# Attention with beacon keys and a gated feed-forward: one rotation of PSUM pairs, a later value phase, and casts moved between engines

## The chip, the cores and the metric

The kernel runs on one core of a Trainium2 chip. The metric is the device time of one launch in microseconds (us), the median of several runs. Its engines work at once and meet at semaphores: TensorE (PE; its weight loads PEld), VectorE (DVE), ScalarE (ACT), GpSimd (POOL) and SyncE (SP, which here only issues DMAs). TensorE writes into PSUM, eight banks of 512 float32 per partition.

## The reference

For 8 batches of 8 heads with 576 queries of 64 dimensions, 16 beacon keys and values are put in front of the 576 others; the mask is causal except for the beacons. The 4608 tokens of 512 values then go through a feed-forward.

```python
scores = scale * np.matmul(q, k_all.transpose(0, 1, 3, 2))
scores = np.where(causal, -1000000000.0, scores)
a = np.exp(scores - scores.max(-1, keepdims=True))
a /= a.sum(-1, keepdims=True) + 1e-09
attn = np.matmul(a, v_all)
x = attn.transpose(0, 2, 1, 3).reshape(B * S, H * D)
return np.maximum(x @ w_gate, 0.0) * (x @ w_val) @ w_out
```

## The kernel before, in words

Everything is in bfloat16, with float32 sums. Scores are computed transposed (keys on the partitions). A *unit* (`Unit`, L363) is one tile of up to 1024 score columns: `qk` (L373) issues its matmuls (L382) into a *pair* of PSUM banks, and `exp` (L387) has ScalarE write the exponentials to SBUF (L390) and, where the tile crosses the diagonal, GpSimd set the forbidden ones to zero (L398, the mask). A *chunk* (`Chunk`, L403) is a set of queries for four heads: `av` (L412) issues the value matmuls and those with ones for the sums (L442), `invert` (L451) has VectorE form the reciprocals (L455), `scale` (L466) has it write the normed result, transposed, to `xT` (L471), and `note` (L476) keeps the range of the reciprocals (L478).

The feed-forward works on tiles of 512 tokens (`Ffn`, L481). `up` (L486) makes one of twelve rows of hidden units: four gate matmuls (L497), a relu by ScalarE (L501, or L512 where gate and value share a pair), four value matmuls (L509) and a product by VectorE (L513). `down` (L515) makes 128 tokens of output with twelve matmuls (L521), which ScalarE copies out (L524) and SyncE stores (L527).

The order is written out by hand: L769 loops over a plan of steps. A step of a batch has two or three units, the chunks whose units the step before finished (`due`), and some `up` and `down` taken from a queue. Batches 0 and 1 have seven steps with two units each, then steps of feed-forward alone; batches 2 to 7 have five steps with 3, 3, 3, 3 and 2 units. In the later batches' steps (L798 to L824) the order on TensorE is two units, the chunk's value phase, the third unit, then `up` and `down`; where no chunk is due, three units and then `up`. PSUM of the later batches (`join_banks`, L736) is two pools: three pairs `p` in turn for scores, gates, values and outputs (one bank of the pair is used for the last three), and one pair `o` for the value phase, or for a step's first unit where no chunk is due; there the first `up` puts gate and value in one pair (`joint`).

Inputs are fetched ahead. For batches 2 to 7 `fetch` (L745) loads three tiles per step (SyncE, L247), casts each `late` steps later (GpSimd, L267 for queries and keys, L262 for values), and one step behind that turns keys and queries by a DMA transpose (SyncE, L272). Raw tiles lie in ten buffers. Batch 1's keys and queries come by casting DMAs issued from GpSimd (L293) and are turned by TensorE (L304); its values are loaded by SyncE and cast by GpSimd (L713). Weights come by casting DMAs issued from GpSimd (`load_w`, L340, issue at L342; `load_wo`, L359, at L360); the last third and `wo` are issued behind a one-element memset by VectorE (L706). So GpSimd's one queue holds masks, casts and issues in program order, and SyncE's holds loads, turns and stores.

Of the kernel before, what the change touches and what calls it, by code (L numbers as in the profile page):

```python
# [161 lines left out]
def kernel(  # L162
# [15 lines left out]
    P = 128  # L178
# [151 lines left out]
    LOADS = ([("k", 0), ("q", 1), ("k", 1), ("q", 2), ("k", 2), ("q", 3), ("k", 3), ("q", 0),  # L330
              ("k", 4), ("q", 4)] + [("v", t) for t in range(NKT)])

    def pair():

        return pools["p"].tile([P, 2, 512], FP32, name="p")

    def bank():
        return pair()[:, 0] if "p" in pools else f_ps.tile([P, 512], FP32, name="f")

    def load_w(dst, src, n0, n1, groups=(0, 1)):  # L340
        for g in groups:
# [61 lines left out]
    class Chunk:  # L403
# [8 lines left out]
        def av(self):  # L412
            batch, g, cis = self.batch, self.g, self.cis
            if batch.b == 0 and g == 1 and cis[0] < 2:
                ab = f_ps.tile([P, 512], FP32, name="f")
                self.os = f_ps.tile([P, 512], FP32, name="f")
            elif batch.b == 1 or batch.b == g == 0:
                ab = o_ps.tile([P, 512], FP32, name="ab")
                self.os = o_ps.tile([P, 512], FP32, name="os")
            else:  # L420
                o = (s_ps.tile([P, 2, 512], FP32, name="s") if batch.b == 0 else
                     pools["o"].tile([P, 2, 512], FP32, name="o"))
                ab, self.os = o[:, 0], o[:, 1]
            self.ab = [ab.rearrange("p (x n) -> p x n", x=2)]
            if len(cis) > 1:
                n = CHUNKS[cis[1]][1]
                self.ab.append(self.os[:, self.n:self.n + 2 * n].rearrange(
                    "p (x n) -> p x n", x=2))
            s0 = 0
            for x, ci in enumerate(cis):  # L430
                cq0, nq, segs = CHUNKS[ci]
                for i, (kt, q0, n, _, _) in enumerate(sorted(segs, key=lambda x: x[0])):
                    e = batch.e.pop((g, ci, kt))
                    kr, stop = min(P, Stot - kt * P), i == len(segs) - 1
                    for part in range(3):
                        for hh in range(4):
                            rows = slice(hh * C, (hh + 1) * C)
                            c0 = (4 * g + hh) * D + part * C
                            w = ones[:kr, :] if part == 2 else batch.v[:kr, kt, c0:c0 + C]
                            o = (self.os[rows, s0:s0 + nq] if part == 2 else  # L440
                                 self.ab[x][rows, part])
                            nc.tensor.matmul(  # L442
                                o[:, q0 - cq0:q0 - cq0 + n], w, e[:kr, 2 * (hh % 2) + hh // 2],
                                start=(x == 0 and i == 0 and part != 1), stop=stop,
                                skip_group_check=True)
# [35 lines left out]
    class Ffn:  # L481
# [1 line left out]
        def __init__(self, m0):  # L483
            self.m0, self.h = m0, None

        def up(self, nf, c0, c1, spare, joint=False):  # L486
            n = c1 - c0
            if self.h is None:
                self.h = fsb.tile([P, NF, M_TILE], BF16, name="hT")
            x = xT[:, :, self.m0 + c0:self.m0 + c1]  # L490
            if joint:
                both = pair()
                g, u = both[:, 0], both[:, 1]
            else:
                g = bank()
            for ki in range(KM):
                nc.tensor.matmul(g[:, :n], wg[:, ki, nf * P:(nf + 1) * P], x[:, ki],  # L497
                                 start=(ki == 0), stop=(ki == KM - 1))
            gs = fsb.tile([P, M_TILE], FP32, name="g")
            if not joint:  # L500
                nc.scalar.activation(gs[:, :n], g[:, :n], AF.Relu)  # L501
            if joint:
                pass
            elif spare and "p" not in pools:
                u = s_ps.tile([P, 2, M_TILE], FP32, name="s")[:, 0]
            else:
                u = bank()
            for ki in range(KM):
                nc.tensor.matmul(u[:, :n], wv[:, ki, nf * P:(nf + 1) * P], x[:, ki],  # L509
                                 start=(ki == 0), stop=(ki == KM - 1))  # L510
            if joint:
                nc.scalar.activation(gs[:, :n], g[:, :n], AF.Relu)  # L512
            nc.vector.tensor_mul(self.h[:, nf, c0:c1], gs[:, :n], u[:, :n])  # L513

        def down(self, ms):  # L515
# [12 lines left out]

        def groups(self, c0, c1, d0, d1):
            t = (c1 - c0) * 8 / 2400  # L530
            return ([("up", t, lambda spare, joint=False, nf=nf: self.up(nf, c0, c1, spare, joint)) for nf in range(NF)]
                    + [("down", 2.6, lambda spare, ms=ms: self.down(ms)) for ms in range(d0, d1)])

    def rows_in_range():
# [6 lines left out]
        return ok  # L541

    def count_rows(ok):
        cnt_ps = pools["o"].tile([P, 2, 512], FP32, name="o")[:1, 0, :1]
# [21 lines left out]
    with tc.manual_schedule():  # L566
# [112 lines left out]
        between[3] = turn_first_tails  # L679
        behind[3] = lambda: [held.pop(0)() for _ in range(2)]  # L680
        after(1, lambda: first.cast("v", 2, pool))
        after(1, lambda: first.cast("v", 3, pool))
        mid[3] = lambda: load_w(wg, moe_w_gate, 256, 768)
        after(3, lambda: load_w(wv, moe_w_val, 256, 768, (0,)))
        after(4, lambda: first.cast("v", 4, pool))
        mid[5] = lambda: [cast_w(wg, raw_g, 256, g, pool) for g in range(2)]
# [23 lines left out]
            load_wo(6, 12)  # L710

        for t in range(NKT):
            after(s2 - 1 + (t + 2) // 2 * (t > 1), lambda t=t: second.cast("v", t, pool))  # L713

        def cast_small(x):
            x.beacon = x.cast_rows(x.beacon, dve)
# [19 lines left out]
        def join_banks():  # L736
            ps_ctx.close()
            pools["p"] = main.enter_context(
                tc.tile_pool(name="p_ps", bufs=3, space=bass.MemoryType.PSUM))
            pools["o"] = main.enter_context(  # L740
                tc.tile_pool(name="o2_ps", bufs=1, space=bass.MemoryType.PSUM))

        after(s2 + 1, close_wide)

# [6 lines left out]
                if u[0] != "v":  # L751
                    at(s + late + 1, lambda u=u: batches[b].turn(*u))

        fetch(2, s2 + 1, 2, True)
        for b in range(3, B):
            fetch(b, BASE[b] - (6 if b == 3 else 5))

        spans = [(m, m + M_TILE) for m in range(0, n_tokens, M_TILE)]
        queue, have, credit = [], 0, 0.0
# [9 lines left out]
        for s, (b, i, quota) in enumerate(plan):  # L769
# [26 lines left out]
                        notes.append(c.note)  # L796

            for j, u in enumerate(units):  # L798
                if len(units) > 2 and chunks and j == 2:
                    units[0].exp()  # L800
                    values()
                if len(units) > 2 and not chunks and j == 0:
                    u.qk(pools["o"].tile([P, 2, 512], FP32, name="o"))
                else:
                    u.qk()
                if j == 0 and s in between:
                    between[s]()
                if j == 0 and s in (3, s2 + 1):
                    values()
                if j == 0 and s == 0:  # L810
                    u.exp()
                    mid[s]()
            if units and s > 0:
                if not (len(units) > 2 and chunks):
                    units[0].exp()
                if s in mid:
                    mid[s]()
            if s in behind:
                behind[s]()
            if s not in (3, s2 + 1) and not (len(units) > 2 and chunks):  # L820
                values()
            if len(units) > 2:
                for u in units[1:]:
                    u.exp()  # L824
            if s == 7:
# [10 lines left out]
                credit -= mine[-1][1]  # L836
            if not mine:
                credit = 0.0
            other = units[1:] if len(units) == 2 else []
            for act_ in acts[:len(acts) // 2]:  # L840
                act_()
            acts = acts[len(acts) // 2:]
# [87 lines left out]
```

## Time and profile before

| | |
|---|---|
| median of 4 runs | 392.68 us (391.47 to 393.93) |
| the profiled execution | 393.93 us, its span 392.1 us |
| TensorE busy | 372.9 us (95%) |
| VectorE, ScalarE, GpSimd busy | 199.9, 190.4, 124.8 us |
| granted TensorE clock | 0.996 of full |
| DMA moved | 50.44 MB, 129 GB/s over the span |
| chain that ended last | 71% TensorE, 10% DMA, 6% GpSimd, 4% SyncE, 4% ScalarE |

The profile is of one execution, with times in us from its start. A row of a timeline names start, busy time, engine, line, operation, output<-input, shape and count, and in brackets how long the engine was idle before it and what ended that. Matmuls overlap, so that their busy times add to more than the clock; the distance from start to start is what they take.

### The profile page before, as it was taken

The page shows a single profiled execution, that of the slowest core. Times are in us where ns is not written, and L with a number is a line of the kernel's source. Part 1 is how long each engine was busy: PE and PEld are TensorE (multiplying, and loading weights), DVE is VectorE, ACT ScalarE, POOL GpSimd, SP SyncE. Part 2 cuts the span into 40 slices and gives each one's busy share as a digit, 9 for nine tenths or more (in the row PEclk, how much of TensorE's full clock was granted, in tenths as well). Part 3 has the DMA queues.
Part 4 walks back from the last instruction along what each step waited for, and adds up shares of the span by engine and source line. Part 5 has one row for each costly group of instructions (what it writes and reads, how often), then busy time and mean ns, then how long its engine had stood idle before and what let it go on. Part 6 is the DMA issues. An engine that isn't in the chain of part 4 may idle for free.

```text
span 392.1 us, 10193 instructions
## 1 busy us (share of the span) xinstructions
PE 372.9 (95%) x4297; PEld 188.1 (48%) x4297; DVE 199.9 (51%) x307; ACT 190.4 (49%) x270; POOL 124.8 (32%) x221
## 2 busy tenths in 40 slices
PE   7889898999979999999999999999999999999995
PEld 3454444544534455545554554555445544444443
DVE  4768466542643575347633674267525765412320
ACT  4763583337645553665356534654455613323321
POOL 1596564323444432352324242325320200000000
PEclk9999999999999999999999999999999999999999
DMA  8999999789869975696568755886210011002002
GB/s 217 215 184 174 194 195 220 153 171 210 140 135 217 200 148 131 169 186 117 108 167 183 146 105 138 181 131 138 79 55 2 2 56 53 2 28 82 1 27 87
DMA packets 148132, 50.44 MB, mean 129 GB/s; under 512 B 133616, under 2 KB 143600, under 8 KB 148080
## 3 DMA queue, kind: packets, MB, share of 16 engines
q1 hardware_dynamic: 139024, 44.48, 52.9%
q0 software_dynamic: 9056, 5.24, 10.0%
q8 instruction: 35, 0.57, 0.6%
q14 instruction: 17, 0.14, 0.1%
HBM read 38.34 MB, written 9.44 MB: 122 GB/s over the span
## 4 chain that ended last, share of the span: by engine, by line
PE 71%; DMA 10%; POOL 6%; SPq 4%; ACT 4%; issue 3%; DVE 1%; ACTq 0%; POOLq 0%
PE p L521 20%; PE p L497 17%; PE p L509 16%; PE o L442 6%; DMA raw<-in_k_dram 4%; PE p L382 4%; DMA raw<-in_v_dram 3%; DMA raw<-in_q_dram 2%; PE f L521 2%; PE f L497 2%; SPq L247 2%; ACT e L390 2%; DMA hwide<-in_k_dram 2%; POOL e L398 1%; PE s L509 1%
## 5 line engine op out<-in xcount | busy, mean ns | idle before, releaser
L513 DVE TENSOR_TENSOR hT<-g,p 128x512 bf16<-128x512 f32 x89 | 61.1, 688 | 108.8 <-PE p L509 72.1
L497 PE MATMUL p<-xT,wg 128*128 128x512 bf16 x356 | 91.5, 379 | 1.0 <-DVE hT L513 0.9
L509 PE MATMUL p<-xT,wv 128*128 128x512 bf16 x356 | 91.3, 379 | 0.0
L398 POOL TENSOR_SCALAR_AFFINE_SELECT e<-e 128x512 bf16<-128x512 bf16 (+2 forms) x80 | 46.2, 600 | 141.1 <-ACT e L390 141.1
L521 PE MATMUL p<-wo,hT 128*128 128x512 bf16 (+1 forms) x396 | 86.6, 376 | 0.0
L501 ACT ACTIVATE g<-p 128x512 f32<-128x512 f32 x82 | 49.3, 601 | 71.4 <-PE p L497 71.4
L390 ACT ACTIVATE e<-p 128x1024 bf16<-128x1024 f32 (+2 forms) x77 | 69.7, 960 | 14.7 <-PE p L382 14.1
L509 PEld LDWEIGHTS <-wv 128*128 128x128 bf16 x432 | 42.2, 98 | 51.4 <-issue 0.5
L521 PEld LDWEIGHTS <-hT 128*128 128x128 bf16 x444 | 42.4, 99 | 50.4 <-issue 3.9
L455 DVE RECIPROCAL r<-o 128x256 f32<-128x256 f32 (+1 forms) x24 | 47.0, 1958 | 34.8 <-PE o L442 34.8
L497 PEld LDWEIGHTS <-wg 128*128 128x128 bf16 x432 | 40.2, 97 | 51.1 <-issue 6.6
L524 ACT COPY ob<-p 128x512 f32<-128x512 f32 (+1 forms) x33 | 18.9, 574 | 67.5 <-PE p L521 64.8
L267 POOL CAST half<-raw 128x512 bf16<-128x512 f32 (+2 forms) x60 | 35.8, 622 | 24.3 <-DMA raw<-in_k_dram 15.0
L442 PEld LDWEIGHTS <-v 128*32 128x32 bf16 (+1 forms) x1408 | 27.1, 97 | 14.4 <-issue 9.6
L442 PE MATMUL o<-e,v 128*32 128x80 bf16 (+4 forms) x1056 | 29.6, 231 | 3.7 <-POOL e L398 2.8
L382 PEld LDWEIGHTS <-kT 64*128 64x128 bf16 x704 | 20.0, 96 | 22.0 <-issue 18.6
L262 POOL CAST v<-raw 128x512 bf16<-128x512 f32 (+1 forms) x40 | 24.9, 648 | 16.0 <-DMA raw<-in_v_dram 16.0
L390 ACT ACTIVATE e<-s 128x1024 bf16<-128x1024 f32 (+2 forms) x28 | 25.7, 967 | 6.3 <-PE s L382 6.3
L442 PE MATMUL o<-e,ones 128*32 128x80 bf16 (+4 forms) x528 | 24.2, 230 | 0.0
L382 PE MATMUL p<-qT,kT 64*128 64x80 bf16 (+3 forms) x476 | 24.1, 230 | 0.0
L497 PE MATMUL f<-xT,wg 128*128 128x512 bf16 x76 | 19.6, 380 | 0.3 <-DMA hwide<-in_k_dram 0.3
L501 ACT ACTIVATE g<-f 128x512 f32<-128x512 f32 x19 | 11.4, 599 | 16.5 <-PE f L497 16.5
(82 smaller groups left out, 249.1 us busy)
## 6 DMA issues: line engine op xcount, KB each, us to landing
out_dram<-ob SPq DMA_DIRECT2D x35, 256.0 KB, 2.3
raw<-in_q_dram SPq DMA_DIRECT2D x25, 256.0 KB, 4.4
raw<-in_v_dram SPq DMA_DIRECT2D x24, 256.0 KB, 4.3
raw<-in_k_dram SPq DMA_DIRECT2D x19, 256.0 KB, 4.4
raw<-in_v_dram SPq DMA_DIRECT2D x8, 224.0 KB, 3.6
wo<-in_moe_w_out_dram POOLq DMA_DIRECT2D x2, 768.0 KB, 12.9
raw<-in_k_dram SPq DMA_DIRECT2D x6, 224.0 KB, 3.5
raw<-in_v_dram SPq DMA_DIRECT2D x8, 160.0 KB, 4.6
```

The costliest lines, as they stand in the source:

```text
L262: copy(self.v[:n, t].rearrange("p (h a d) -> p h a d", a=2, d=C), raw[:n].rearrange("p (h d a) -> p h a d", a=2, d=C))
L267: copy(h[:n], raw[:n])
L382: nc.tensor.matmul(self.s[:, a, c + j * n:c + (j + 1) * n], kT[rows, 2 * g + j, k0:k0 + P], qT[rows, 2 * g + j, q0:q0 + n], start=True, st ...
L390: nc.scalar.activation(e[:, :k * 4 * n].rearrange("p (k a x) -> p a k x", k=k, a=2), self.s[:, :, :k * 2 * n].rearrange("p a (k x) -> p a ...
L398: nc.gpsimd.affine_select(out=cols[:, :, :m], in_=cols[:, :, :m], pattern=[[0, 4], [1, m]], compare_op=ALU.is_ge, fill=0.0, base=base, cha ...
L442: nc.tensor.matmul(o[:, q0 - cq0:q0 - cq0 + n], w, e[:kr, 2 * (hh % 2) + hh // 2], start=(x == 0 and i == 0 and part != 1), stop=stop, ski ...
L455: nc.vector.reciprocal(self.r[:, :self.n], self.os[:, :self.n])
L497: nc.tensor.matmul(g[:, :n], wg[:, ki, nf * P:(nf + 1) * P], x[:, ki], start=(ki == 0), stop=(ki == KM - 1))
L501: nc.scalar.activation(gs[:, :n], g[:, :n], AF.Relu)
L509: nc.tensor.matmul(u[:, :n], wv[:, ki, nf * P:(nf + 1) * P], x[:, ki], start=(ki == 0), stop=(ki == KM - 1))
L513: nc.vector.tensor_mul(self.h[:, nf, c0:c1], gs[:, :n], u[:, :n])
L521: nc.tensor.matmul(o[:, n], self.h[:, nf, ms * P:(ms + 1) * P], wo[:, nf, n], start=(nf == 0), stop=(nf == NF - 1))
```

## The change

PSUM of batches 2 to 7 becomes four pairs of names p0 to p3, and `pair` takes the one that was least recently taken. The value phase takes such a pair too, and single banks (`bank`) spare it until the next step's value phase begins. All units of a step are issued ahead of its value phase. The shared pair of gate and value goes. The casts of batch 2 come three steps behind their loads (two before), those of batch 3 two (one before), and their turns one step later with them. In batch 0 the cast of the fourth values goes from the end of step 1 to the middle of step 3, and the load of gate weights from there to the end of step 3. Batch 1's first two value tiles are cast by VectorE.

```diff
-    def pair():
-        return pools["p"].tile([P, 2, 512], FP32, name="p")
+    pairs, kept = list(range(4)), []
+
+    def pair(spared=()):
+        k = next(k for k in pairs if k not in spared)
+        pairs.remove(k)
+        pairs.append(k)
+        return pools["p"].tile([P, 2, 512], FP32, name=f"p{k}")
 
     def bank():
-        return pair()[:, 0] if "p" in pools else f_ps.tile([P, 512], FP32, name="f")
+        return pair(kept)[:, 0] if "p" in pools else f_ps.tile([P, 512], FP32, name="f")
...
-                o = (s_ps.tile([P, 2, 512], FP32, name="s") if batch.b == 0 else
-                     pools["o"].tile([P, 2, 512], FP32, name="o"))
+                if batch.b == 0:
+                    o = s_ps.tile([P, 2, 512], FP32, name="s")
+                else:
+                    o = pair()
+                    kept.append(pairs[-1])
...
-            if joint:
-                both = pair()
-                g, u = both[:, 0], both[:, 1]
-            else:
-                g = bank()
+            g = bank()
...
-        after(1, lambda: first.cast("v", 3, pool))
-        mid[3] = lambda: load_w(wg, moe_w_gate, 256, 768)
+        mid[3] = lambda: first.cast("v", 3, pool)
+        after(3, lambda: load_w(wg, moe_w_gate, 256, 768))
...
-            after(s2 - 1 + (t + 2) // 2 * (t > 1), lambda t=t: second.cast("v", t, pool))
+            after(s2 - 1 + (t + 2) // 2 * (t > 1), lambda t=t: second.cast("v", t, pool if t > 1 else dve))
...
-                tc.tile_pool(name="p_ps", bufs=3, space=bass.MemoryType.PSUM))
-            pools["o"] = main.enter_context(
-                tc.tile_pool(name="o2_ps", bufs=1, space=bass.MemoryType.PSUM))
+                tc.tile_pool(name="p_ps", bufs=1, space=bass.MemoryType.PSUM))
...
-        fetch(2, s2 + 1, 2, True)
+        fetch(2, s2 + 1, 3, True)
         for b in range(3, B):
-            fetch(b, BASE[b] - (6 if b == 3 else 5))
+            fetch(b, BASE[b] - (6 if b == 3 else 5), 2 if b == 3 else 1)
...
-                if len(units) > 2 and chunks and j == 2:
-                    units[0].exp()
-                    values()
-                if len(units) > 2 and not chunks and j == 0:
-                    u.qk(pools["o"].tile([P, 2, 512], FP32, name="o"))
-                else:
-                    u.qk()
+                u.qk()
...
             if units and s > 0:
-                if not (len(units) > 2 and chunks):
-                    units[0].exp()
+                units[0].exp()
...
-            if s not in (3, s2 + 1) and not (len(units) > 2 and chunks):
+            kept.clear()
+            if s not in (3, s2 + 1):
                 values()
-            if len(units) > 2:
+            if units and b >= 2:
                 for u in units[1:]:
                     u.exp()
...
-                if kind == "up" and j == 0 and len(units) > 2 and not chunks:
-                    run(False, True)
-                    continue
```

More of the change, by code (lines that the diff above doesn't have):

```diff
@@ L484, in __init__, with up @@
             self.m0, self.h = m0, None
-        def up(self, nf, c0, c1, spare, joint=False):
+        def up(self, nf, c0, c1, spare):
             n = c1 - c0
@@ L499, in up @@
             gs = fsb.tile([P, M_TILE], FP32, name="g")
[L500 to L504, printed above, removed]
+            nc.scalar.activation(gs[:, :n], g[:, :n], AF.Relu)
+            if spare and "p" not in pools:
                 u = s_ps.tile([P, 2, M_TILE], FP32, name="s")[:, 0]
@@ L510, in up @@
                                  start=(ki == 0), stop=(ki == KM - 1))
-            if joint:
-                nc.scalar.activation(gs[:, :n], g[:, :n], AF.Relu)
             nc.vector.tensor_mul(self.h[:, nf, c0:c1], gs[:, :n], u[:, :n])
@@ L530, in groups @@
             t = (c1 - c0) * 8 / 2400
-            return ([("up", t, lambda spare, joint=False, nf=nf: self.up(nf, c0, c1, spare, joint)) for nf in range(NF)]
+            return ([("up", t, lambda spare, nf=nf: self.up(nf, c0, c1, spare)) for nf in range(NF)]
                     + [("down", 2.6, lambda spare, ms=ms: self.down(ms)) for ms in range(d0, d1)])
@@ L543, in count_rows @@
     def count_rows(ok):
-        cnt_ps = pools["o"].tile([P, 2, 512], FP32, name="o")[:1, 0, :1]
+        cnt_ps = pair()[:1, 0, :1]
         nc.tensor.matmul(cnt_ps, ok, ones[:, :1], start=True, stop=True)
@@ L838 @@
                 credit = 0.0
-            other = units[1:] if len(units) == 2 else []
+            other = units[1:] if b in (0, 1) else []
             for act_ in acts[:len(acts) // 2]:
```

## The prediction

> **What bounds the kernel now.** I read the table by stages first, cut at the moments when a batch's first score unit starts.
>
> ```profile
> 40.00:88.00 48.00, 44.47 (x564) 22.36 (x562) 26.73 (x41) 24.14 (x35) 23.41 (x39) 1.00 1.03 188
> 88.00:128.00 40.00, 35.30 (x493) 18.32 (x493) 17.49 (x21) 24.07 (x31) 18.16 (x33) 0.96 0.86 178
> 209.20:249.72 40.52, 40.33 (x497) 20.48 (x496) 21.99 (x31) 21.55 (x30) 14.42 (x27) 1.00 0.68 147
> ```
>
> The first column after the stretch is its length, the next TensorE's busy time; the last three are granted clock, DMA share, GB/s. From 128 on TensorE is busy 40.33 of 40.52 us per batch: it is the bound, and only its gaps and the entries between kinds of matmul are left. Before 128 some 14 us are idle and the clock dips once. So I read TensorE's timeline for every gap (in brackets: idle before, and who ended it).
>
> ```profile
> 23.20 0.40 PE L442 MATMUL f<-e,v 128*32 128x256 bf16 x8 [0.77 <-POOL e L398]
> 49.47 0.39 PE L442 MATMUL ab<-e,v 128*32 128x240 bf16 x8 [1.19 <-POOL e L398]
> 61.94 1.46 PE L521 MATMUL f<-wo,hT 128*128 128x512 bf16 x6 [0.84 <-DMA wo<-in_moe_w_out_dram]
> 65.44 0.40 PE L442 MATMUL ab<-e,v 128*32 128x256 bf16 x8 [0.81 <-POOL e L398]
> 103.11 0.39 PE L442 MATMUL o<-e,v 128*32 128x240 bf16 x8 [0.90 <-DVE xT L471]
> 109.23 0.30 PE L442 MATMUL o<-e,v 128*32 128x128 bf16 x8 [0.36 <-POOL e L398]
> 116.32 0.33 PE L442 MATMUL o<-e,v 80*32 80x80 bf16 x8 [2.48 <-POOL e L398]
> 117.18 6.45 PE L521 MATMUL p<-wo,hT 128*128 128x512 bf16 x24
> 128.16 1.02 PE L497 MATMUL p<-xT,wg 128*128 128x512 bf16 x4 [0.19 <-DVE hT L513]
> ```
>
> Five of these end at a causal mask (L398) on GpSimd. GpSimd's own timeline says why the last was late:
>
> ```profile
> 111.97 0.60 POOL L267 CAST half<-raw 64x512 bf16<-64x512 f32 x1 [1.67 <-DMA raw<-in_q_dram]
> 114.63 1.21 POOL L262 CAST v<-raw 128x512 bf16<-128x512 f32 x2 [2.06 <-DMA raw<-in_v_dram]
> 115.79 0.47 POOL L398 TENSOR_SCALAR_AFFINE_SELECT e<-e 128x320 bf16<-128x320 bf16 x1
> ```
>
> The mask's input was ready at 109.4 (ScalarE's exps of 107.83), but it stood in line behind batch 3's casts, and those waited for loads. The chain of waits runs through the same load, cast and mask.
>
> **The change, part by part.** From the instruction order of both builds: ScalarE's order differs in one swap, TensorE's only in where value phases stand, and GpSimd's and SyncE's in casts and turns.
>
> *Batch 0's fourth values after the first mask, gate weights after the last.* At 19.19 GpSimd cast v3 (landed 19.13), then two masks to 21.0, two weight issues (20.95, 1.54 us), then the mask that TensorE needed, 22.51 to 23.15. Now the two masks (their exp ended 17.88) fit in the 1.53 us in which GpSimd sat idle before 19.19, v3 follows, the needed mask ends at 19.83 + 0.64 = 20.5: the 0.77 gap goes. VectorE's unbroken string from 23.93 to 27.83, which the first up-projection at 27.35 needs, moves with it: 0.8 us. The weight issues go about 0.5 us earlier, what follows them 1.0.
>
> *Batch 1's first two values by VectorE.* On GpSimd they took 1.25 us (47.63) ahead of the mask that TensorE awaited at 49.47: that gap of 1.19 goes. VectorE's casts of 128x512 take 0.43 us (L289), this strided one at most the 0.65 of GpSimd's L262: 0.9 to 1.3 us, in VectorE's idle 1.97 us before 46.67. Behind them stands the product at 46.67, for which TensorE waits at 47.41; cost there 0 if the values have landed by 44.5, up to 1 us else. I take 0, since the next gap covers it: at 61.94 TensorE waits for wo, which came 15.1 us after its issue (46.81) with the DMA engines saturated (share 1.03). So of all gained so far only what moves wo's landing survives. Its issue is gated by VectorE's memset at 42.77, behind TensorE's turns at 40.63, which wait for loads that GpSimd now issues 1.0 earlier. Bounds 0 and 1.0; I take 0.85, as the transfers were idle for 2 us at 27 to 29 waiting for exactly those issues.
>
> *Casts of batches 2 and 3 one step later.* Masks now precede casts that wait for loads. The gaps at 65.44 (0.81), 109.23 (0.36) and 116.32 go. The last is worth 2.65 us (the last matmuls would have started at 113.67). And the 24 down-projections behind it took 6.39 us against 5.29 elsewhere, with the granted clock at 0.50 in 116 to 118 and 0.64 in 118 to 120: 1.10 more. The Trainium skill speaks against this term: its page "TensorE: Matmul & The Clock Gate", section "Part 1: The HAM clock gate (the \"warmup\" mystery)", lets the clock fall to half only after an idle window of about 3.4 us. By that rule an idle of 2.48 us does not dip and nothing is to be had here (sum 4.96); by the row it did, behind a phase of small matmuls, and waits of 0.77 to 1.19 us did not. The row decides: 1.10.
>
> The price is on SyncE: turns (L272) now stand behind later loads. For batch 2 the turn of q3, issued until 80.78, gets 2.55 us of loads and stores put in front (2.08 for v2 to v4, 0.47 for a store), less the 0.85 lead: 82.5, landing 1.5 later at 84 (turns take 2.7 from issue to landing, 1.2 of it issue). TensorE wants it at 88.91 - 1.66 = 87.25. Covered. For batch 3 the first units want q3 by 112.31 - 1.8 = 110.5; it was issued until 108.86, gets 2.94 us of loads in front, gains the lead, and loses 1.6 and 1.0 us of waits for casts inside two turns: 108.3 to 111, landing 109.8 to 112.4. The last turn, q4, is wanted at 123.9 - 5.6 = 118.3; between 88 and 125 SyncE waited 10.6 us for GpSimd, so it lands between 114 (no waits left, held by a store that needs the second down-projection) and 122 (all left). The middle, 118, costs about 0.3; bounds 0 and 4.
>
> *Four pairs, least recently used; value phase behind three score units.* Each run of score matmuls pays an entry of about 0.11 us: four of 256 columns alone took 0.32 us (214.48 to 214.80), eight 0.54. One run fewer in three steps of a batch: 0.32 us. The pair that gate and value shared is gone; at 128.16 and its like the third gate waited 0.35 (start to start) for VectorE's product, and the new order makes it wait for ScalarE's relu of the first, 0.4 us earlier than needed: 0.35 gained, less 0.05 as the first value tile now waits for an exp that ends as it wants to start. Added waits: in the third and fourth steps the value phase takes the pair of the last up-projection's product.
>
> ```profile
> 212.92 0.69 DVE L513 TENSOR_TENSOR hT<-g,p 128x512 bf16<-128x512 f32 x1 [1.04 <-PE p L509]
> 213.21 0.40 PE L442 MATMUL o<-e,v 128*32 128x256 bf16 x8
> 221.99 0.69 DVE L513 TENSOR_TENSOR hT<-g,p 128x512 bf16<-128x512 f32 x1 [1.04 <-PE p L509]
> 222.36 0.39 PE L442 MATMUL o<-e,v 128*32 128x240 bf16 x8
> ```
>
> The product ends at 213.61, and TensorE started 0.06 after such an end at 209.20. The value phase, moved 0.21 behind a third unit, would want 213.42: 0.25 lost. In the next step product 222.68 against 222.56: 0.18, and 0.1 more as the wait sits on the weight load. Behind it queue the next up-projections; nobody else is late, as ScalarE already has its three exps. Per batch 0.32 + 0.30 - 0.53 = about 0.1, at most 0.6; five batches: 0.75 taken, -1 to 2. In batch 2 the 0.90 wait at 103.11 stays, now at the second score unit: 0.25 for its third step's value phase and 0.23 for the score units that now run behind that wait, against entries of 0.32, lose 0.16. The gap of 0.85 at batch 2's first unit (88.91) stays: the built program has its first score matmul wait for the same last product.
>
> **Sum.** 0.85 + 0.81 (65.44) + [0.36 + 2.65 + 1.10 - 0.16 - 0.3 = 3.65] + 0.75 = 6.06 us. The profiled execution took 393.93 (span 392.1): 387.9. It is the slowest of the four runs, 1.25 above the median, so 386.6 against 392.68. A difference of 0.5% (2 us) is about what this kernel's measurement can tell from none.
>
> **Rivals.** (1) The sum, 386.6: 0.58. (2) The turns take GpSimd's place: TensorE waits about 2 us for q4 of batch 3 near 118 and the clock dips as it did at 116: 3.1 given back, 389.7. For it: SyncE issues without a pause from 90 to 122 now; against: a third of that was waiting for casts. 0.20. (3) The pairs do not come free: each of the twelve value-phase waits 0.35 longer than the 0.25 above, 4 us: 390.6. For it: VectorE's reciprocals (1.76 and 2.16 us) stand ahead of products; against: at 212.92 VectorE had been idle 1.04. 0.12. (4) Slower: batch 2's loads of q4 and of the first values, now ahead of all its turns, are throttled as those issued at 53.84 (4.54 us) and 58.47 (3.43) were while wo was in flight. At 4 us each instead of 2.9 for all, q3's turn lands near 95, not 84, TensorE stands 7.4 us at 87.25 and pays 1.4 for the clock: 8.8 against 6.06, 395.4. It decides against the change if that turn lands after 93.3; against it, loads from 62 on took 0.8 to 1.2 each, wo having landed. 0.10.
>
> Range: (2) and (3) at the upper end, wo's lead of 1.0 and no wait for turns at the lower, with 2 us for the pairs: 383.8 to 391.2. Faster by over 0.5% (under 390.7): all of (1), most of (2) and half of (3), 0.79; within: 0.13; slower: 0.08.
>
> **What would show it.** Right: no GpSimd-ended gap over 0.3 us in TensorE's value phases; clock 1.00 from 110 to 125, 24 down-projections in 5.3 us there; batch period 40.2 to 40.5 after 128; third gate of a batch's second step without gap; value phases of the third and fourth steps with a VectorE-ended gap of 0.2 to 0.3. Wrong: a gap in front of score matmuls (L382, now another line) ended by a turn; wo's wait grown past 0.84 by all that was gained ahead of it; a batch period over 40.7.

## The result, and the profile after

The changed kernel takes 391.44 us in the median of 42 runs (388.58 to 393.77), the kernel before 392.75 in 63 runs: a ratio of 0.9967, 95% interval 0.9953 to 0.998. That is 0.8 to 1.8 us of gain where 6.1 were forecast; the time lies just above the range given. The profiled execution of after took 392.99 us (span 391.3, clock 0.989), slower than 37 of the 42.

The executions of one kernel scatter here with a standard deviation of 0.6 to 2.0 us. So a profile below shows a mechanism, and the ratios of many runs say what it is worth.

First the table by stages (columns as before); the third row is a batch of the later part.

```profile
40.00:88.00 48.00, 45.84 (x579) 23.16 (x578) 27.85 (x44) 24.81 (x37) 22.76 (x38) 1.00 1.00 191
88.00:128.00 40.00, 34.05 (x475) 18.06 (x474) 16.20 (x19) 22.22 (x30) 17.48 (x31) 0.91 0.91 173
192.23:232.48 40.25, 39.99 (x505) 20.73 (x497) 21.83 (x30) 21.50 (x31) 14.42 (x27) 1.00 0.69 147
```

The first stage became better: TensorE is busy 45.84 us instead of 44.47. A batch takes 40.25 instead of 40.52. But the stage between, where most of the gain was to come from, became worse: 34.05 instead of 35.30, the clock 0.91 instead of 0.96. TensorE's timeline of after shows where:

```profile
50.31 0.61 PE L511 MATMUL f<-xT,wv 128*128 128x512 bf16 x2 [0.23 <-DMA wv<-in_moe_w_val_dram]
51.26 0.60 PE L511 MATMUL f<-xT,wv 128*128 128x512 bf16 x2 [0.34 <-DMA wv<-in_moe_w_val_dram]
86.29 0.83 PE L388 MATMUL p<-qT,kT 64*128 64x256 bf16 x12 [0.85 <-DVE hT L513]
114.23 1.46 PE L388 MATMUL p<-qT,kT 64*128 64x256 bf16 x12 [4.52 <-DMA qT<-half]
117.67 6.59 PE L521 MATMUL p<-wo,hT 128*128 128x512 bf16 x24
213.41 0.40 PE L451 MATMUL p<-e,v 128*32 128x256 bf16 x8 [0.16 <-DVE hT L513]
```

All five gaps that GpSimd's masks ended are gone. In their place batch 3's first scores wait 4.52 us for a turn, that of q3, and run at half clock behind it. (L388 is the scores' line now, L451 the values', L511 the up-projections' value line; L521, L247, L262, L267 and L272 are what they were.) No mask is late any more; it now stands ahead of the casts that wait for loads, as intended:

```profile
105.38 0.61 POOL L267 CAST half<-raw 80x512 bf16<-80x512 f32 x1 [0.23 <-DMA raw<-in_k_dram]
106.73 0.48 POOL L404 TENSOR_SCALAR_AFFINE_SELECT e<-e 128x320 bf16<-128x320 bf16 x1 [0.74 <-ACT e L396]
109.39 0.60 POOL L267 CAST half<-raw 64x512 bf16<-64x512 f32 x1 [2.18 <-DMA raw<-in_q_dram]
```

The cast of q3 itself had ended by 101.8. What came late is its turn on SyncE's queue (start, time that the queue was held, what was issued; of the ten loads at the head only the first, the longest and the last are shown):

```profile
90.09 0.56 SPq L247 DMA_DIRECT2D raw<-in_beacon_k_dram  x1
92.40 3.34 SPq L247 DMA_DIRECT2D raw<-in_q_dram  x1
99.74 1.41 SPq L247 DMA_DIRECT2D raw<-in_k_dram  x1
101.33 1.20 SPq L272 DMA_TRANSPOSE kT<-half  x1
102.61 1.67 SPq L272 DMA_TRANSPOSE qT<-half  x1
104.38 1.22 SPq L272 DMA_TRANSPOSE kT<-half  x1
105.65 0.65 SPq L247 DMA_DIRECT2D raw<-in_q_dram  x1
106.35 0.61 SPq L247 DMA_DIRECT2D raw<-in_beacon_v_dram  x1
107.00 1.97 SPq L247 DMA_DIRECT2D raw<-in_v_dram  x2
109.07 1.23 SPq L272 DMA_TRANSPOSE qT<-half  x1
110.39 1.21 SPq L272 DMA_TRANSPOSE kT<-half  x1
111.70 1.22 SPq L272 DMA_TRANSPOSE qT<-half  x1
```

The last row is q3's. In the kernel before, the same load and the same turn stood so:

```profile
92.18 1.58 SPq L247 DMA_DIRECT2D raw<-in_q_dram  x1
107.64 1.22 SPq L272 DMA_TRANSPOSE qT<-half  x1
```

In after, from the first load of batch 3 at 90.09 to the end of q4's turn at 121.93 SyncE issues 29 DMAs without a pause, 31.8 us. TensorE wants q3 at 109.71.

### The profile page after: what moved, and what is told of

It is laid out like the page before. It is cut to its first block, busy times and chain, and to the rows that moved or that the text cites. A ratio compares the mean times of both kernels' runs of the same rounds, so it can differ in the third digit from the quotient of the medians.

```text
span 391.3 us, 10201 instructions
## 1 busy us (share of the span) xinstructions
PE 372.5 (95%) x4297; PEld 190.2 (49%) x4297; DVE 198.9 (51%) x309; ACT 190.0 (49%) x270; POOL 124.3 (32%) x219
## 4 chain that ended last, share of the span: by engine, by line
PE 83%; DMA 7%; DVE 3%; POOL 3%; issue 1%; SPq 1%; ACT 1%; DVEq 0%
PE p L521 20%; PE p L502 20%; PE p L511 20%; PE p L451 7%; PE p L388 3%; DMA wv<-in_moe_w_val_dram 3%; PE f L521 3%; DVE hT L513 3%; PE f L502 2%; PE s L388 1%; DMA hwide<-in_k_dram 1%; PE s L511 1%; PE f L304 1%; PE f L511 1%; POOL e L404 1%; PE ab L451 1%
## 5 line engine op out<-in xcount | busy, mean ns | idle before, releaser
L511 PE MATMUL p<-xT,wv 128*128 128x512 bf16 x356 | 91.3, 379 | 0.0
L505 ACT ACTIVATE g<-p 128x512 f32<-128x512 f32 x89 | 52.8, 603 | 71.4 <-PE p L502 71.3
L521 PE MATMUL p<-wo,hT 128*128 128x512 bf16 (+1 forms) x396 | 86.7, 377 | 0.0
L396 ACT ACTIVATE e<-p 128x1024 bf16<-128x1024 f32 (+2 forms) x84 | 75.2, 966 | 17.6 <-PE p L388 17.6
L464 DVE RECIPROCAL r<-p 128x256 f32<-128x256 f32 (+1 forms) x24 | 47.0, 1958 | 43.5 <-PE p L451 43.5
L511 PEld LDWEIGHTS <-wv 128*128 128x128 bf16 x432 | 42.0, 98 | 53.1 <-DMA wv<-in_moe_w_val_dram 2.2
L521 PEld LDWEIGHTS <-hT 128*128 128x128 bf16 x444 | 42.4, 98 | 48.6 <-issue 1.8
L267 POOL CAST half<-raw 128x512 bf16<-128x512 f32 (+2 forms) x60 | 36.2, 628 | 12.5 <-DMA raw<-in_k_dram 6.3
L388 PEld LDWEIGHTS <-kT 64*128 64x128 bf16 x704 | 21.1, 97 | 27.4 <-issue 23.8
L451 PEld LDWEIGHTS <-v 128*32 128x32 bf16 (+1 forms) x1408 | 28.3, 99 | 9.7 <-issue 4.5
L451 PE MATMUL p<-e,v 128*32 128x80 bf16 (+4 forms) x1056 | 30.2, 235 | 1.5 <-DVE hT L513 1.0
L388 PE MATMUL p<-qT,kT 64*128 64x80 bf16 (+3 forms) x528 | 23.5, 231 | 6.6 <-DMA qT<-half 4.5
L262 POOL CAST v<-raw 128x512 bf16<-128x512 f32 (+1 forms) x38 | 23.7, 648 | 10.3 <-DMA raw<-in_v_dram 10.2
L451 PE MATMUL p<-e,ones 128*32 128x80 bf16 (+4 forms) x528 | 25.0, 234 | 0.0
L451 PEld LDWEIGHTS <-ones 128*32 128x32 bf16 (+1 forms) x704 | 19.7, 100 | 0.2
```

The costliest lines, as they stand in the source:

```text
L262: copy(self.v[:n, t].rearrange("p (h a d) -> p h a d", a=2, d=C), raw[:n].rearrange("p (h d a) -> p h a d", a=2, d=C))
L267: copy(h[:n], raw[:n])
L388: nc.tensor.matmul(self.s[:, a, c + j * n:c + (j + 1) * n], kT[rows, 2 * g + j, k0:k0 + P], qT[rows, 2 * g + j, q0:q0 + n], start=True, st ...
L396: nc.scalar.activation(e[:, :k * 4 * n].rearrange("p (k a x) -> p a k x", k=k, a=2), self.s[:, :, :k * 2 * n].rearrange("p a (k x) -> p a ...
L451: nc.tensor.matmul(o[:, q0 - cq0:q0 - cq0 + n], w, e[:kr, 2 * (hh % 2) + hh // 2], start=(x == 0 and i == 0 and part != 1), stop=stop, ski ...
L464: nc.vector.reciprocal(self.r[:, :self.n], self.os[:, :self.n])
```

## The experiments

Each ratio is to runs of the kernel before that were taken beside it on the same chip, with its 95% interval; "second step" is the start of batch 3's second step on TensorE in the profiled execution (123.56 before, 124.19 after).

**The pairs alone**: the changed kernel with all moved casts and turns back in their old places.

```diff
-        fetch(2, s2 + 1, 3, True)
+        fetch(2, s2 + 1, 2, True)
...
-            fetch(b, BASE[b] - (6 if b == 3 else 5), 2 if b == 3 else 1)
+            fetch(b, BASE[b] - (6 if b == 3 else 5))
```

(and the early edits to batches 0 and 1 undone as below in "no front".)

> The kernel after with its moved casts and turns undone: the pairs in turn and the value phase behind three score units alone. Theory (the gain that is left is that of the pairs): batches of 40.25 us in place of 40.52 after 128, five of them, so 1.3 us less than before, a ratio near 0.9967; the mask wait of 2.5 us near 116 stays as before. Rival (the pairs only trade one wait for another and the gain comes from the early casts): within 0.3 us of before.

Measured: 392.34 us, ratio 0.9964 (0.9934 to 0.9994). The pairs, with the later value phase, are worth 1.3 us by the difference of the spans' last parts as well: from the block of 24 down-projections that starts at 151.52 before to the end it is 240.6 us before and 239.3 here. Every later kernel with pairs has 239.3 to 239.6 there, those without 240.6 to 240.8. So the pairs alone gain as much as the whole change. The mask wait of 2.48 us stayed, and the clock dipped behind it, as it did behind one of 1.18 us at 48.74:

```profile
48.74 0.48 PE L451 MATMUL ab<-e,v 128*32 128x240 bf16 x8 [1.18 <-POOL e L404]
50.31 1.89 PE L502 MATMUL f<-xT,wg 128*128 128x512 bf16 x4
115.96 0.26 PE L451 MATMUL p<-e,v 80*32 80x80 bf16 x8 [2.48 <-POOL e L404]
116.18 7.04 PE L521 MATMUL p<-wo,hT 128*128 128x512 bf16 x24
```

**The front alone**: the kernel before with the early edits and batch 2's casts three steps late.

```diff
-        after(1, lambda: first.cast("v", 3, pool))
-        mid[3] = lambda: load_w(wg, moe_w_gate, 256, 768)
+        mid[3] = lambda: first.cast("v", 3, pool)
+        after(3, lambda: load_w(wg, moe_w_gate, 256, 768))
...
-        fetch(2, s2 + 1, 2, True)
+        fetch(2, s2 + 1, 3, True)
```

(and batch 1's first two value casts on VectorE.)

> The kernel before with the early edits alone: batch 0's fourth values, the gate weights, batch 1's values on VectorE and batch 2's casts a step later; batch 3 and the pairs as before. Theory (SyncE's one queue sets when batch 3 is ready, and it gained no lead): batch 2 starts 2.6 us earlier, but the mask wait near 116 grows by as much, from 2.5 to about 5 us; the time stays within 0.5 us of before. Rival (every removed gap counts): 2.6 us less, a ratio of 0.9934.

Measured: 392.78 us, ratio 0.995 (0.9917 to 0.9984). TensorE's rows:

```profile
114.08 0.26 PE L442 MATMUL o<-e,v 80*32 80x80 bf16 x8 [2.48 <-POOL e L398]
114.62 5.35 PE L521 MATMUL p<-wo,hT 128*128 128x512 bf16 x24
```

Batch 2 starts at 86.16 instead of 88.91, the mask wait is the 2.48 us of before and not longer, and the second step starts at 119.91. In this execution SyncE began batch 3's loads at 87.70, not near 90, so the lead was kept; this execution (390.82 us) is the third fastest of its twelve. The theory that all of the lead is waited away did not hold here. And the clock stayed at 1.00 behind the same 2.48 us.

**Batch 3's later casts alone** in the kernel before.

```diff
-            fetch(b, BASE[b] - (6 if b == 3 else 5))
+            fetch(b, BASE[b] - (6 if b == 3 else 5), 2 if b == 3 else 1)
```

> The kernel before with batch 3's casts and turns one step later alone. Theory: the two mask waits (0.36 and 2.48) go and a wait of the first score matmuls of batch 3 for a DMA turn of about 2.2 us takes their place, ended near 114; less idle, so the dip of the clock is milder or gone: 0.4 to 1.9 us less than before. Rival (the turns were ready in time at the old pace, and only the faster front made them late): no wait for a turn, 3 to 4 us less.

Measured: 392.56 us, ratio 0.9977 (0.9941 to 1.0012).

```profile
113.18 0.61 PE L382 MATMUL p<-qT,kT 64*128 64x256 bf16 x8 [2.12 <-DMA qT<-half]
```

This wait stands where the mask's stood, no dip follows, and the second step starts at 120.47. By the ratio the edit is worth between 2.3 us and nothing: one wait takes the place of the other.

**The wait filled**: the changed kernel with 18 matmuls on `wo` in front of batch 3's first scores, into the pair that those then overwrite.

```diff
-                u.qk()
+                if b == 3 and i == 0 and j == 0:
+                    fill = pair()
+                    for _ in range(18):
+                        nc.tensor.matmul(fill[:, 0], wo[:, 0, :P], wo[:, 0, :512], start=True, stop=True)
+                    u.qk(fill)
+                else:
+                    u.qk()
```

> The kernel after with eighteen matmuls of 512 columns on weights already there, put into the pair of batch 3's first score unit ahead of it; their results are overwritten. They take 3.9 us inside the 4.5 us wait. Theory (the wait costs twice, once as idle and once by the clock): the wait is still ended by the turn near 114, the clock stays at 1.00, the score and value phases take 1.9 instead of 3.4 us and the 24 down-projections 5.3 instead of 6.5: 2.8 us less than the kernel after. Rival (the slow matmuls after the wait have another cause, such as the transfers then running): as the kernel after.

Measured: 391.31 us, ratio 0.9925 (0.9893 to 0.9958).

```profile
109.57 4.05 PE L800 MATMUL p<-wo 128*128 128x512 bf16 x18
114.00 0.83 PE L388 MATMUL p<-qT,kT 64*128 64x256 bf16 x12 [0.38 <-DMA qT<-half]
115.89 5.35 PE L521 MATMUL p<-wo,hT 128*128 128x512 bf16 x24
123.21 0.39 PE L388 MATMUL p<-qT,kT 64*128 64x80 bf16 x12 [1.44 <-DMA qT<-half]
```

The turn lands when it did, but the clock stays at 1.00: from the scores to the end of the 24 down-projections 7.17 us pass (114.00 to 121.17) instead of 9.96 (114.23 to 124.19). The dip costs 2.8 us. Half of what is saved is then waited for the next turn, q4's.

**Batch 3 back to one step**: the changed kernel without that edit (the reverse of the diff under "Batch 3's later casts alone").

> The changed kernel with one edit undone: batch 3's casts and turns stand one step behind their loads again, as before, while batch 2's stay at three. Theory (the two halves of the change spoil each other: the front's lead is real and lasts, the pairs' 0.27 us a batch lasts, and only the turn of q3 behind the value loads on SyncE, with the clock's dip behind it, ate the rest): batch 3's second step starts near 120 us instead of 124.19, with a mask wait of about 2.5 us near 114 and no wait for q3's turn; 4 us under the changed kernel, a ratio to before of 0.985 to 0.989. Rival (the turn's wait only takes the place of the mask waits, and any lead of the front is lost in the transition): second step at 123 to 124, ratio 0.994 to 0.998. Rival (the clock dips behind the 2.5 us mask wait here as in the kernel before): second step near 121.5, ratio 0.990 to 0.993.

Measured: 391.34 us, ratio 0.9962 (0.9933 to 0.999), so the changed kernel's own time. Its profiled execution was the fastest of its twelve (388.96) and shows a second step at 119.78 and a mask wait of 1.83 us; the other eleven say that this is not its usual course. The theory falls, and by its ratio the first rival stands: with or without the edit, about as much is lost. Where a usual execution loses it, no trace shows.

**Turns before values**: the changed kernel, batch 3's values loaded and cast one step later.

```diff
-                s = s0 + j // 3
+                s = s0 + j // 3 + (b == 3 and u[0] == "v")
```

> The changed kernel, with batch 3's five value tiles loaded and cast one step later; all casts and turns of its queries and keys stand as in the changed kernel. Theory (the turn of q3 is late by its place on SyncE's queue, behind the loads of k and v tiles): three issues of together 3.3 us leave its front, so it is issued by about 109.7 instead of 112.9 and lands near 111.2; batch 3's first scores wait 1.5 us instead of 4.5, TensorE's clock does not dip (2.8 us), and the second step starts at 118.5 to 119.5, where q4's turn, which has not become earlier, ends a wait of up to 3 us; 2 to 4 us under the changed kernel, ratio to before 0.987 to 0.992. Rival (the turn is late by the transfers and not by the queue: the DMA engines are full then, and the same bytes have to move): the wait stays over 3.5 us, the clock dips, ratio 0.995 to 0.998.

Measured: 393.66 us, ratio 1.0024 (1.0 to 1.0049).

```profile
111.90 5.35 PE L521 MATMUL p<-wo,hT 128*128 128x512 bf16 x24
117.19 0.60 PE L388 MATMUL p<-qT,kT 64*128 64x128 bf16 x12
122.35 0.59 PE L388 MATMUL p<-qT,kT 64*128 64x80 bf16 x12 [4.56 <-DMA qT<-half]
```

```profile
106.61 2.08 SPq L272 DMA_TRANSPOSE qT<-half  x1
```

The queue's part was right: q3's turn is issued at 106.61, lands at 109.8, and TensorE doesn't wait for it. The second step starts at 117.19, 7.0 us ahead of after. But it then stands 4.56 us for q4's turn and pays for the clock again (0.50 from 122 to 126). All is given back, and more.

**Only the first six tiles one step late** (k0 to q3), the other nine two.

```diff
-        def fetch(b, s0, late=1, held=False):
+        def fetch(b, s0, late0=1, held=False):
...
+                late = 1 if b == 3 and j < 6 else late0
```

> The changed kernel with only batch 3's first six tiles (k0 to q3) cast and turned one step behind their loads, and the other nine two steps behind. Theory (it is the turn's extra step that makes q3 late, not batch 2's): T q3 is issued by about 107 to 109, batch 3's first scores wait 0.5 us at most, the mask of batch 2's last part has only casts with landed tiles ahead of it and waits under 0.7 us; second step at 117.5 to 119, then a wait for q4's turn of 2 to 4 us as with the filled wait (1.44 us there); ratio to before 0.986 to 0.991. Rival (the later tiles' turns come so late that all of it is given back at q4): ratio 0.993 to 0.997.

Measured: 393.76 us, ratio 1.0001 (0.997 to 1.0032); the rival. The first scores don't wait, but the second step waits for the turns of k and q tiles (0.96 and 0.29 us, then 1.82 for the exps behind them), and behind these waits the clock dips to 0.50 in 126 to 128.

**Only the values late**: queries and keys one step behind their loads as before, the values loaded and cast one step later.

```diff
-                s = s0 + j // 3
+                s = s0 + j // 3 + (b == 3 and u[0] == "v")
...
-            fetch(b, BASE[b] - (6 if b == 3 else 5), 2 if b == 3 else 1)
+            fetch(b, BASE[b] - (6 if b == 3 else 5))
```

> The changed kernel with batch 3's queries and keys one step behind their loads as before, and only its values moved: loaded and cast one step later. Theory (both waits come from the five value tiles: their casts stood ahead of batch 2's last mask on GpSimd, and their loads ahead of the turns on SyncE): neither the mask wait of 2.5 us near 114 nor a turn's wait over 0.7 us appears, the clock stays at 1.00, and the second step starts at 117 to 118.5, 6 to 7 us ahead of the changed kernel; ratio to before 0.979 to 0.985. Rival (q4's turn cannot land before 121, whatever stands ahead of it): the second step waits until 121 for it, ratio 0.985 to 0.990. Rival (the values come too late for batch 3's first value phase): a new wait for v of over 1 us near 150 and a ratio over 0.990.

Measured: 388.78 us, ratio 0.9874 (0.9832 to 0.9916; six runs), 3.6 us under the changed kernel by the ratios. "Batch 3 back to one step", on the same chip, differs from it only in where the values stand: 391.34 us, 2.6 more.

```profile
109.18 0.30 PE L451 MATMUL p<-e,v 128*32 128x128 bf16 x8 [0.77 <-POOL e L404]
112.16 0.83 PE L388 MATMUL p<-qT,kT 64*128 64x256 bf16 x12
114.10 5.35 PE L521 MATMUL p<-wo,hT 128*128 128x512 bf16 x24
121.17 0.39 PE L388 MATMUL p<-qT,kT 64*128 64x80 bf16 x12 [1.18 <-DMA qT<-half]
```

```profile
107.24 1.22 SPq L272 DMA_TRANSPOSE qT<-half  x1
114.96 2.23 SPq L247 DMA_DIRECT2D raw<-in_v_dram  x2
```

q3's turn is issued at 107.24, and v0 and v1 are loaded at 114.96, behind the turns. Neither the mask wait of 2.5 us nor the turn's wait appears, and the clock is 1.00. One wait of 1.18 us for q4 is left until 121.17, as the first rival said, and the second step starts at 119.39, later than the theory had it; a mask wait of 1.31 us at 98.69 is new. So both waits came from the same five tiles: where their casts stood ahead of a mask on GpSimd, the mask waited; where the turns were put behind their loads on SyncE, the scores did. All fourteen profiles agree on the second half: from batch 3's first load to the issue of q3's turn pass 20.1 to 22.0 us in the five where value loads stand ahead of it on SyncE's queue, and 16.0 to 18.3 in the nine others.

**And q4's turn early**: the same, with q4's turn directly behind those of k3, q0 and k4.

```diff
-                    at(s + late + 1, lambda u=u: batches[b].turn(*u))
+                    at(s + late + (b != 3 or u != ("q", 4)), lambda u=u: batches[b].turn(*u))
```

> The kernel with batch 3's values one step later and its queries and keys one step behind their loads, and besides that the turn of q4 one step earlier, directly behind those of k3, q0 and k4 and ahead of the loads of v0 and v1. Theory (SyncE's queue orders it): three loads and a store of together some 3.5 us leave the front of q4's turn; it is issued near 114.5 instead of 117.9 and lands before 118; the wait of 1.18 us at batch 3's second step goes; 1.2 us under the kernel with the late values, ratio to before 0.981 to 0.986. Rival (q4's turn is held by the transfers, not by its place): no change to that kernel, 0.986 to 0.990.

Measured: 388.73 us, ratio 0.9898 (0.9879 to 0.9918). The turn is issued at 113.48 instead of 117.90 and its wait is gone, but the ratio (of six runs) isn't below that of the kernel with late values; the intervals overlap, and whether the 1.2 us are worth anything stays open. In the profiled execution batch 2 began at 90.78, after waits of 0.78 and 1.81 us for weights and a dip of the clock behind them (0.50 in 54 to 58), all ahead of anything that this edit touches.

**Values by GpSimd's queue**: the changed kernel, but batch 3's six value loads are issued by GpSimd.

```diff
+                eng = nc.gpsimd if x == "v" and b == 3 else nc.sync
```

> The changed kernel with one thing else: batch 3's six value loads are issued by GpSimd's queue instead of SyncE's. Steps, bytes, casts and turns stay. Theory (the turns were late by SyncE's queue): 3.3 us of issues leave the front of the turn of q3 and 5.1 us the front of that of q4; q3's turn lands near 111.5 instead of 114.2, the scores wait 2 us at most instead of 4.5, the clock does not dip, q4's turn causes no wait over 1 us; second step near 118.5 to 120, 4 to 5 us under the changed kernel, ratio to before 0.984 to 0.988. Rival (the DMA engines are full, and any queue would give the same): the wait for q3's turn stays over 3.5 us, ratio 0.994 to 0.999. What GpSimd pays for six issues may delay batch 2's masks by up to 1 us.

Measured: 393.47 us, ratio 1.0021 (0.9993 to 1.0048).

```profile
100.93 1.75 POOL L248 DMA_DIRECT2D raw<-in_v_dram  x2
106.06 2.52 POOL L248 DMA_DIRECT2D raw<-in_v_dram  x3
```

```profile
107.44 1.23 SPq L273 DMA_TRANSPOSE qT<-half  x1
```

```profile
115.02 1.47 PE L389 MATMUL p<-qT,kT 64*128 64x256 bf16 x12 [5.82 <-DMA qT<-half]
```

The theory fell: q3's turn is issued 4.3 us earlier than in after (3.3 counted from the first load, as expected), and lands later. It needed 7.4 us from issue to landing instead of 2.4. GpSimd's loads ran at the same time, and the mean DMA share from 98 to 110 was 1.27 (0.99 in after). The places freed on SyncE were of no use here, where the transfers that had been in front ran beside the turns.

**Thin values**: the changed kernel, the value loads of batch 3 with 2 of 8 heads, a quarter of the bytes.

> The changed kernel, but batch 3's value loads bring only the first 2 of 8 heads (a quarter of the bytes; the other heads' values of batch 3 are set to zero by VectorE, so that batch's output is not the reference's). Issues, their order on SyncE, casts and turns stay. It asks whether the turns are late by the places that the six value loads take on SyncE's queue or by the bytes that they put into the DMA engines. Theory of bytes (which the slow turns of the kernel with GpSimd's value loads speak for): 0.75 of 0.5 MB is missing ahead of the turn of q3, at some 200 GB/s 1.9 us; the three issues shrink from 2.6 to 1.5 us as well; q3's turn lands by 111.5 to 112.3 instead of 114.1, the wait falls under 2.5 us, the clock stays, and the time is 3 to 4 us under the changed kernel, ratio to before 0.986 to 0.990. Theory of places: the turn lands after 112.8, the wait stays over 3 us, and the time is at most 1 us under the changed kernel, ratio 0.993 to 0.997.

Measured: 390.4 us, ratio 0.9937 (0.991 to 0.9964), about 1.2 us under the changed kernel by the ratios, whose intervals overlap: the theory of places by the time, though not by its signs. Counted from the first load of batch 3, the turn of q3 is issued after 20.6 us (87.66 to 108.27) instead of 21.6 (90.09 to 111.70), and other kernels with this order and all bytes needed 20.1 to 22.0, so that no saving by the fewer bytes shows beyond the scatter. The profiled execution, the fastest of its twelve (388.03 us), had no wait for q3 at all: its loads started 2.4 us earlier.

**No front**: the changed kernel with the early edits undone.

```diff
-        mid[3] = lambda: first.cast("v", 3, pool)
-        after(3, lambda: load_w(wg, moe_w_gate, 256, 768))
+        after(1, lambda: first.cast("v", 3, pool))
+        mid[3] = lambda: load_w(wg, moe_w_gate, 256, 768)
...
-            after(s2 - 1 + (t + 2) // 2 * (t > 1), lambda t=t: second.cast("v", t, pool if t > 1 else dve))
+            after(s2 - 1 + (t + 2) // 2 * (t > 1), lambda t=t: second.cast("v", t, pool))
```

> The changed kernel with the early edits undone: batch 1's first two value casts again on GpSimd, the fourth value cast and the weight loads of batch 0 in their old places. Everything later is the changed kernel's. Theory (SyncE's queue, which does not start batch 3's loads earlier with the front than without it, sets when the turn of q3 lands, so the front's lead is waited away): batch 2 starts 1.7 to 2.6 us later, the wait for q3's turn is shorter by the same, and the time is the changed kernel's within 0.4 us, ratio to before 0.995 to 0.998. Rival (the front's 1.7 us is a gain of its own, and the rest of the change costs 1.7 more than it brings but for the pairs): ratio 1.000 to 1.002.

Measured: 390.99 us, ratio 0.9967 (0.9945 to 0.9988), the changed kernel's own.

```profile
113.86 0.83 PE L388 MATMUL p<-qT,kT 64*128 64x256 bf16 x12 [1.72 <-DMA qT<-half]
115.75 5.35 PE L521 MATMUL p<-wo,hT 128*128 128x512 bf16 x23
```

Batch 2 starts 2.45 us later (88.74; part of this is a dip of the clock from 50 to 54 that after does not have), the wait for q3 is 2.80 shorter (1.72), and the turn lands when it did. The front's lead is waited away in the changed kernel.

## Why the prediction was wrong

The direction held; the size did not. Taking the steps in their order:

*The front (forecast 0.85 + 0.81).* Batch 2's first unit came 2.62 us earlier in the pair of profiles. Over all profiles its start is 86.47 in the median of ten kernels with the early edits, 88.45 in four without: 2.0, so the sum for TensorE was nearly right. The wait for `wo` is absent in after and 0.44 to 1.12 in some others, with waits of 0.2 to 1.8 us for `wv` that were not forecast. What failed is the half-sentence that SyncE "gains the lead": SyncE's first load of batch 3 stands at 90.09 against 89.97 before, and by the medians of the same profiles it gained 0.5 us (89.3 against 89.75). SyncE's string does not begin there: from batch 2's first load (50.71 in after, 51.36 before) its issues hold the queue for 36.4 of the 39.4 us to batch 3's first, before for 35.6 of 38.6, so there was little idle time for a lead to shorten.

*Batches 2 and 3 (forecast 3.65).* The gains named there came: the masks' waits of 0.36 and 2.48 are gone. The step that failed is the price on SyncE, "108.3 to 111, landing 109.8 to 112.4", and with it the 0.3 us for all waits for turns (bounds 0 and 4). q3's turn was issued until 112.9 and landed at 114.1. Two terms were mis-sized. The lead of 0.85 was 0. And the ten loads that now stand ahead of the first turn were taken over at what they had held the queue before, 7.7 us together; they held it 10.4 us (0.4 to 3.3 each), until 101.2. The longest held it while the DMA share was 0.99, but before, at a share of 1.15, the same load held it 1.58 us, so why they took longer stays open. The waits for casts inside turns did go: the first six turns held the queue 7.8 us instead of 10.1. TensorE was ready at 109.71 and not at 110.5. So the wait was 4.52 us, with a dip behind it of 2.8, which the sum did not hold for any turn. The forecast's second step was due at 118.3 and came at 124.19: 4.52 + 2.79 - 0.96 (more front than forecast) - 0.3 makes 6.05 of these 5.9 us. The 118 for q4's turn rested on 10.6 us in which SyncE waited for GpSimd, of which about half was to go; the same view of after still has 10.2 us, and q4's turn landed at 123.0, past the later bound of 122. Rival (2) had the right mechanism, turns in GpSimd's place and a dip, but named q4's turn and 3.1 us.

*The clock.* The dip was forecast to go; it grew. I followed the row of before (2.48 us idle, then 0.50). The runs show both: 2.48 us brought a dip in before and in the pairs alone, and none with the front alone; 2.12 and 1.83 brought none; 4.52, 4.56 and 5.82 all did. Shorter ones sometimes did too, against the forecast's reading that waits of 0.77 to 1.19 do not: behind the 1.18 us at 48.74 the pairs alone ran at 0.50 in 50 to 52, while the kernel before ran at 1.00 behind the same wait of 1.19; and behind 0.96, 0.29 and 1.82 us the kernel with six early tiles ran at 0.50. The Trainium skill, page "TensorE: Matmul & The Clock Gate", section "Part 1: The HAM clock gate (the "warmup" mystery)", has an idle window of about 3.4 us that runs freely. The long waits agree with that; the dips after 2.48 us and less do not, and there the measurement stands. The 1.10 us was not to be had in every execution of before: of the 104 taken beside the experiments, 15 have a mean clock of 1.00, so no dip at all. The term was too large by a part that no run here isolates.

*Pairs and value phase (forecast 0.75, -1 to 2).* Right within its bounds: 1.3 us. Step by step in a batch, before and after, from start to start: first step 7.28 and 7.17; second 8.15 and 7.80 (the third gate's gap gone); third 9.07 and 9.20, fourth 9.00 and 9.06, which hold the waits for the product. The sum is -0.27; forecast -0.1, at most -0.6. The VectorE-ended gap is 0.16 in the third step's value phase; the fourth shows none.

*Rivals (3) and (4)* did not come. Batch 2's turns were in time: its first unit waits 0.85 us for a product as before.

So of 6.06 us forecast, the pairs' part arrived, and the rest, 5.3, was spent in front of and behind q3's turn. That most of it was there to be had is shown by the late values: 0.9874 is 4.9 us under before (3.3 to 6.6), with the same front and the same pairs.

What stays open: why the front alone still kept 0.6 to 3.3 us, while it is worth nothing in the changed kernel (the intervals just allow one value near 1 us), and why SyncE's issues take so unequally long: from batch 2's first load to batch 3's they hold the queue 34.3 to 37.5 us in the ten profiles with the same front, and so batch 3's loads start anywhere from 87.7 to 91.9.

## What to carry to other kernels

When an order is changed to spare a full engine, add up the queue that pays for it as a stage of its own, from its first instruction to the one that somebody awaits. Here SyncE's 29 issues took 31.8 us where TensorE's work took 30.5 (86.70 to 117.19 in the kernel with the turns before the values, no turn awaited), so SyncE was the bound of that stage, and a lead of TensorE's, or a mask in time, only made the next wait longer. What helped was not another queue but order: the transfers whose results are needed last were put behind all those needed first.

## What the runs showed of the hardware

A DMA transpose of 128x512 held SyncE's queue for 1.2 us at least, and landed 2.3 to 5.6 us after its issue beside SyncE's own loads, but up to 7.4 us beside loads from GpSimd's queue. A load's issue held it for 0.4 to 3.3 us among batch 3's loads in after (DMA share 0.34 over the first four, 0.99 over the longest), and for 4.5 us at 53.84 before, at a share of 1.22. The clock's answer to an idle of 2.48 us differed between executions with the same wait, and so it did to one of 1.2 us.
